# Row scatters of a group queued and issued between units of visits, in a fused convolution and expert-routing kernel

## The chip, the cores and the metric

The kernel runs on one core of one Trainium2 chip. The metric is device time in microseconds (us) of one execution; lower is better. A core has five engines that run side by side, each through its own instruction queue in order: PE (matrix multiply, with PEld for its weight loads), DVE (vector), ACT (scalar), POOL (GpSimd, which here issues indirect transfers) and SP (which here issues plain transfers). They wait for one another through semaphores.

## The reference

```python
# convolution: 7 taps per token, softmax weights per token and head
w = exp(weight_gen - max) ; w = w / (sum(w) + 1e-09)
out = np.einsum('bshk,bskhg->bshg', w, x_unf)      # x_unf: the token and its 6 predecessors
x = out.reshape(B * S, D)                          # 23040 tokens, D = 192
# two-level routing: 4 groups of 4 experts
g_idx = argmax(x @ w_group) ; g_w = its softmax weight
e_idx = argmax(x @ w_expert[g_idx]) ; e_w = its softmax weight
# the expert of each token: w1 192x1024, w2 1024x192
h = np.maximum(x[tokens] @ w1[g, e], 0.0)
out[tokens] = (g_w * e_w)[:, None] * (h @ w2[g, e])
```

## The kernel before

The 23040 tokens are cut into 15 groups of 12 columns of 128 tokens. For each group the front of the kernel (`front`, `softmax`, `conv`, `logits`, `ranks`) computes the convolution on DVE, the routing logits on PE, and on DVE each token's place in a DRAM table `rows` that is sorted by expert. Then POOL scatters the twelve columns into `rows`: `scatter_row`, one indirect transfer of 128 rows of 194 floats each, line L488. In the rows below a scatter is `rows<-xrow,posi`.

The experts' work is cut into visits. A visit takes one, two or three blocks of 128 rows of one expert and is done in units (four for two blocks, eight for three): first matrix product (`gemm1`, L872) into `ph`, ReLU on ACT into `hh` (L878, L883), second product (`gemm2`, L910 to L913) into `py`, then `y` (ACT L919 or DVE), and POOL writes the result rows to their tokens with an indirect transfer `out<-y,xb` (L927), one per block, 189 in all. SP's `load` fetches what a visit needs: its rows `xb` (L744), the weights of the first product `raw` (L757 and L764, three transfers of 512, 256 and 256 KB, called a triple below), and those of the second, `wc` (L768). ACT and DVE then split a triple into the three parts of `wa` (ACT casts L781 and L790, DVE L805).

A table `ROUNDS` says after which group which visits become possible: a round may begin when its group's ranks and the `table` of visits made from them are there. `ready(n)` tells whether visit n's round has come; `arrive` holds the planned time of its rows. The order of the instructions is fixed when the program is written: a planner keeps a clock per engine (`clk`, advanced by `run`), `blocks` runs through the units of all visits, and after each unit `fill` pulls steps of the front until DVE's planned clock is ahead. `pump` issues the loads that are asked for and ready; `need` pulls the front until a visit's round is there. PE, ACT, DVE and SP execute in just that written order. POOL's queue is ordered by the framework's scheduler, from the same program.

In `ranks` the twelve scatters are written one after another, directly behind the last DVE step of the group. After the last group, `table` also writes 16 blocks of padding into `rows` (`rows<-pad`, L543, on POOL).

Of the kernel before, what the change touches and what calls it, by code (L numbers as in the profile page):

```python
# [20 lines left out]
LATE = (1.0, 3.0, 3.0)  # L21
AHEAD = (1.0, 1.0, 2.5)
HURRY = 12
WHOLE = 13
SINGLE = tuple((k,) for k in range(7))
MIXED = ((0, 1), (2,), (3,), (4,), (5,), (6,))
# [11 lines left out]
def conv_moe_kernel(ctx: ExitStack, tc: tile.TileContext, x, wgen, w_group, w_expert, w1, w2, out):  # L38
# [13 lines left out]
    SC = 6  # L52
# [13 lines left out]
    ENDS = [r[0] for r in ROUNDS]  # L66
# [6 lines left out]
    FIRST = ENDS[0]  # L73
# [146 lines left out]

    new_raw = [ring(f"raw{i}", m, [P, n]) for i, (n, m) in enumerate(((F, 2), (F, 2), (NFT * D, 1)))]

    state = {"slots": False, "open": False, "unit": 0, "starve": False, "ph": 0, "hold": False}

    def ph_tile(k, shape):
        return ps_h.tile(shape, F32, name=f"ph{k}")
# [9 lines left out]
    def run(eng, cost, *deps):  # L236
        clk[eng] = max([clk[eng]] + [d + HOP for d in deps]) + cost
        return clk[eng]
# [10 lines left out]
    def round_of(g):  # L249
        return next(r for r in range(NR) if g < ENDS[r])  # L250
# [164 lines left out]
    def ranks(g, o, ls, tls):  # L415
        s0, n = COL[g], WIDTHS[g]
        xrow = o.xrow
        for c, row in enumerate(xrow):
            nc.vector.tensor_copy(out=row.bitcast(I32)[:, :, D + 1:D + 2], in_=ii[:, s0 + c * SC:s0 + (c + 1) * SC].unsqueeze(2))
        yield 0.3  # L420
        yield tls
        ohg, exg = yield from first_max(ls[:, :, 0:G], n, "g")
        sel = rt.tile([P, SG, EG, G], F32, name="sel")[:, 0:n]
        nc.vector.tensor_tensor(
            out=sel, in0=ls[:, :, G:].rearrange("p s (g e) -> p s e g", g=G),
            in1=ohg.unsqueeze(2).broadcast_to([P, n, EG, G]), op=ALU.mult)
        yield 0.3
        le = rt.tile([P, SG, EG], F32, name="le")[:, 0:n, :]
        nc.vector.tensor_reduce(out=le, in_=sel, axis=AX.X, op=ALU.add)
        yield 0.3  # L430
        ohe, exe = yield from first_max(le, n, "e")
        ohs = rt.tile([P, SG, EG], F32, name="ohs")[:, 0:n, :]
        nc.vector.tensor_tensor(out=ohs, in0=ohe, in1=sgn4.broadcast_to([P, n, EG]), op=ALU.mult)
        smg = rt.tile([P, SG, 1], F32, name="smg")[:, 0:n, :]
        nc.vector.tensor_reduce(out=smg, in_=exg, axis=AX.X, op=ALU.add)
        yield 0.26
        oh = rt.tile([P, SG, G, EG], BF16, name="oh")[:, 0:n]
        nc.vector.tensor_tensor(
            out=oh, in0=ohg.unsqueeze(3).broadcast_to([P, n, G, EG]),
            in1=ohs.unsqueeze(2).broadcast_to([P, n, G, EG]), op=ALU.mult)  # L440
        ohf = oh.rearrange("p s g e -> p s (g e)")
        nc.vector.tensor_scalar(out=smg, in0=smg, scalar1=1e-9, scalar2=None, op0=ALU.add)
        yield 0.3
        yield NEXT
        t12 = ps_l.tile([P, 2, SG * NE], F32, name="pl")[:, :, 0:n * NE]
        t1 = t12[:, 0, :].rearrange("p (s e) -> p s e", e=NE)
        t2 = t12[:, 1, :].rearrange("p (e s) -> p e s", e=NE)
        nc.tensor.matmul(t1, lhsT=tri, rhs=ohf, start=True, stop=True)
        nc.tensor.matmul(t2, lhsT=ones, rhs=ohf.rearrange("p s e -> p e s"), start=True, stop=True)
        tt = run("pe", 0.4, clk["dve"])  # L450
        sme = rt.tile([P, SG, 1], F32, name="sme")[:, 0:n, :]
        nc.vector.tensor_reduce(out=sme, in_=exe, axis=AX.X, op=ALU.add)
        yield TINY
        nc.vector.scalar_tensor_tensor(out=smg, in0=sme, scalar=1e-9, in1=smg, op0=ALU.add, op1=ALU.mult)
        yield NEXT
        yield Until(tt + LATE[0])
        pre = rt.tile([P, NE * SG], F32, name="pre")[:, 0:NE * n].rearrange("p (e s) -> p e s", s=n)
        nc.vector.tensor_copy(out=pre[:, :, 1:n], in_=t2[:, :, 0:n - 1])
        nc.vector.tensor_copy(out=pre[:, :, 0:1], in_=cnt)
        yield 0.35  # L460
        for c, row in enumerate(xrow):
            nc.vector.reciprocal(out=row[:, :, D:D + 1], in_=smg[:, c * SC:(c + 1) * SC, :])
        yield TINY
        nc.vector.tensor_tensor_scan(
            out=pre.rearrange("p e s -> p (e s)"), data0=smask[n].rearrange("p e s -> p (e s)"),
            data1=pre.rearrange("p e s -> p (e s)"), initial=0.0, op0=ALU.mult, op1=ALU.add)
        yield 0.3
        rk = sel.rearrange("p s e g -> p s (e g)")
        nc.vector.tensor_tensor(out=rk, in0=pre.rearrange("p e s -> p s e"), in1=t1, op=ALU.add)
        nc.vector.tensor_tensor(out=cnt, in0=pre[:, :, n - 1:n], in1=t2[:, :, n - 1:n], op=ALU.add)  # L470
        yield 0.4
        nc.vector.tensor_tensor(out=rk, in0=rk, in1=ohf, op=ALU.mult)
        yield 0.3
        ps = rt.tile([P, SG], F32, name="pos")[:, 0:n]
        nc.vector.tensor_reduce(out=ps.unsqueeze(2), in_=rk, axis=AX.X, op=ALU.add)
        yield 0.3
        pi = rt.tile([P, SG], I32, name="posi", bufs=2)[:, 0:n]
        nc.vector.scalar_tensor_tensor(out=pi, in0=ps, scalar=-1.0, in1=ps, op0=ALU.mult, op1=ALU.max)
        yield TINY
        for s in range(n):  # L480
            run("pool", 1.28, clk["dve"])
            scatter_row(pi[:, s:s + 1], xrow[s // SC][:, s % SC, :], round_of(g))
        if g + 1 in ENDS:
            yield from table(round_of(g))
        o.routed = True

    def scatter_row(idx, src, r):
        written_once(nc.gpsimd.indirect_dma_start(  # L488
# [11 lines left out]
    tabs, arrive = {}, {}  # L500
# [99 lines left out]
        for h in range(2):  # L600
            nc.gpsimd.dma_start(out=rows[NROW + h * BK:NROW + (h + 1) * BK, :].rearrange("(p t) c -> p t c", t=2), in_=pad2)

    scoring, ranking = [], []
    slow = [[halves(), None]]

    def front():
        side = []
        set_up()
        load_group(1)
        next(slow[0][0])  # L610
        yield from softmax(0)

        def pace(g):
            return 99 if g <= FIRST else HURRY if g < MAIN + 3 else 8 if g in ENDS else 2

        def beside(g, n):
            rush = g >= FIRST and not grp[FIRST - 1].routed
            if g >= FIRST and not rush:
                for q in list(slow):
                    yield from move(slow, q, 1)  # L620
            for q in side[:1]:
                if not rush:
                    yield from move(side, q, 3)
            yield from routing(g)

        def routing(g):
            if ranking:
                yield from move(ranking, ranking[0], pace(g))
            if scoring and (not ranking or g < FIRST):
                yield from move(scoring, scoring[0], pace(g) if scoring[0][2].chunks == 2 or g >= FIRST - 1 else 3)  # L630

        def settle(g):
            while not grp[g].routed:
                qs = ranking or scoring
                q = qs[0]
                yield from move(qs, q, 99)
                if qs and qs[0] is q and q[1] is not None:
                    yield Until(q[1][1]) if q[1][0] == "time" else NEXT

        for g in range(ENDS[-1]):  # L640
            o = grp[g]
            o.routed = False
            scoring.append([logits(g, o), None, o])
            for n, c in enumerate(conv(g, o)):
                yield c
                if n == (2 if state["slots"] else 0) and 1 <= g < ENDS[-1] - 1:
                    load_group(g + 1)
                if n >= (12 if state["slots"] else 4) and not o.ahead and g + 1 < ENDS[-1] and g != FIRST - 1:
                    o.ahead = True
                    side.append([softmax(g + 1), None])  # L650
                yield from beside(g, n)
                if g == FIRST - 1 and n in (7, 8):
                    if n == 7:
                        soft = softmax(FIRST)
                    yield next(soft)
            if g == FIRST - 1:
                for n, c in enumerate(soft):
                    yield c
                    yield from beside(g, n)
            yield from finish_all(side)  # L660
            if g:
                yield from settle(g - 1)
        yield from settle(ENDS[-1] - 1)
# [54 lines left out]
    nmain = len(order)  # L718

    def ready(n):  # L720
        return order[n][:2] in arrive

    def plain(n):
        return order[n][1] == 1
# [207 lines left out]

    def need(n):
        while not ready(n):
            state["starve"] = True
            more = step() is not False
            assert more or ready(n)
        state["starve"] = False
# [13 lines left out]
    def blocks(n0, n1, paced):  # L952
# [92 lines left out]
        for i in range(len(units) + LAG):  # L1045
# [25 lines left out]
            if i < len(units):  # L1071
# [7 lines left out]
                for job in list(jobs):  # L1079
# [7 lines left out]
                    work_split(job)  # L1087
                    did += 1
                state["unit"] += 1
            flush()  # L1090
            if paced:
                fill(clk["pe"] + AHEAD[0 if cur.plain else 1 if cur.o.whole else 2])
# [48 lines left out]
```

## Time and profile before

| | |
|---|---|
| median of 3 runs | 1333.68 us (1323.01 to 1336.16) |
| profiled execution | 1335.81 us |
| its span in the trace | 1334.1 us |
| mean granted clock of PE | 0.951 |
| PE busy | 1192.9 us (89%) |
| DVE busy | 950.5 us (71%) |
| ACT busy | 640.1 us (48%) |
| POOL busy | 455.6 us (34%) |

The profiled execution is 2.1 us above the median. 1.7 us of it lie outside the span. Busy time counts the instructions that compute or issue an indirect transfer; an engine that is not busy is waiting for data, for another engine, or to be given its next instruction. The granted clock of PE has two levels, 2.4 GHz (1.0) and 1.2 GHz (0.5); a mean between them says what share of a stretch was at the lower one.

### The profile page before, as it was taken

The numbers are of one execution on the slowest core, as the hardware profiler recorded it, in microseconds if no ns is written. First come the engines' busy times: TensorE is split into PE (matmuls) and PEld (weight loads), VectorE is DVE, ScalarE is ACT, GpSimd is POOL, SyncE is SP. The second block draws the span as 40 slices with busy tenths as digits, with TensorE's granted clock in tenths as the row PEclk, the third lists the DMA queues.
The fourth block names the chain that finished last, engine by engine and source line by source line (L and its number), as shares of the span: only waits on it lengthen the run. The fifth ranks groups of instructions, "written<-read, shape, count | busy, mean of one in ns | idle before, by whom it ended". The sixth has DMA issues, their size and how long they took to land. (4 is left out here: it accounts for less than half of the span.)

```text
span 1334.1 us, 23736 instructions
## 1 busy us (share of the span) xinstructions
PE 1192.9 (89%) x8165; PEld 1104.5 (83%) x8165; DVE 950.5 (71%) x1660; ACT 640.1 (48%) x1232; POOL 455.6 (34%) x442
## 2 busy tenths in 40 slices
PE   5776877798999999999989798989786999999995
PEld 3444877688998989898989697989686999999995
DVE  8897776768988979798978597888633146655662
ACT  1223334344555555455545454645343466556652
POOL 6232331415253525344533415252416312112221
PEclk9988998788999999899999899999887999999998
DMA  9238789555878767677776666545436665565551
GB/s 258 85 120 275 239 213 287 190 197 172 265 224 278 215 236 225 228 223 253 229 237 213 217 196 209 188 155 168 158 88 216 197 205 149 154 176 165 151 164 39
DMA packets 78851, 261.94 MB, mean 196 GB/s; under 512 B 14669, under 2 KB 29559, under 8 KB 76928
## 3 DMA queue, kind: packets, MB, share of 16 engines
q1 hardware_dynamic: 59544, 220.85, 54.4%
q0 software_dynamic: 19056, 39.20, 8.8%
q8 instruction: 66, 1.08, 0.3%
q14 instruction: 65, 0.53, 0.1%
q10 hardware_dynamic: 120, 0.28, 0.1%
HBM read 216.92 MB, written 44.23 MB: 196 GB/s over the span
## 5 line engine op out<-in xcount | busy, mean ns | idle before, releaser
L872 PE MATMUL ph<-xh,wa 128*128 128x256 f32 (+1 forms) x1896 | 477.0, 321 | 8.1 <-issue 7.4
L910 PE MATMUL py<-wc,hh 128*128 128x192 f32 x2272 | 440.2, 334 | 34.4 <-issue 17.5
L927 POOL DMA_INDIRECT out<-y,xb x189 | 222.1, 1175 | 706.3 <-ACT y L919 449.5
L910 PEld LDWEIGHTS py<-wc,hh 128*128 128x128 f32 x2272 | 379.2, 196 | 40.6 <-issue 22.3
L872 PE MATMUL ph<-xl,wa 128*128 128x256 f32 (+1 forms) x1264 | 360.4, 300 | 8.1 <-issue 8.1
L878 ACT ACTIVATE hh<-ph 128x512 f32<-128x512 f32 (+2 forms) x320 | 175.9, 550 | 366.5 <-PE ph L872 258.4
L872 PEld LDWEIGHTS ph<-xh,wa 128*128 128x128 f32 x1896 | 329.5, 194 | 17.9 <-issue 16.4
L488 POOL DMA_INDIRECT rows<-xrow,posi x180 | 202.1, 1123 | 152.6 <-issue 65.9
L287 DVE TENSOR_TENSOR pr<-xin,wt 128x1152 f32<-128x1152 f32 x186 | 249.0, 1351 | 4.3 <-PE ph L328 2.0
L872 PEld LDWEIGHTS ph<-xl,wa 128*128 128x128 f32 x1264 | 243.4, 193 | 9.5 <-issue 9.5
L305 DVE TENSOR_TENSOR xrow<-xrow,pr 128x1152 f32<-128x1152 f32 x144 | 194.9, 1353 | 0.6
L805 DVE TENSOR_TENSOR wa<-raw,wa 128x1024 fp32r<-128x1024 f32 x79 | 96.5, 1221 | 127.8 <-ACT wa L781 111.7
L805 DVE SCALAR_TENSOR_TENSOR pr<-ph,hh 128x384 fp32r<-128x384 f32 (+1 forms) x120 | 68.8, 574 | 89.0 <-ACT hh L883 84.0
L805 DVE TENSOR_TENSOR xl<-tpx,xh 128x512 fp32r<-128x512 f32 (+1 forms) x99 | 62.8, 634 | 61.5 <-ACT xh L852 50.6
L883 ACT ACTIVATE hh<-ph 128x384 fp32r<-128x384 f32 (+1 forms) x120 | 61.1, 510 | 79.8 <-PE ph L872 70.5
L912 PE MATMUL py<-wc,hh 128*128 128x384 f32 x272 | 87.2, 362 | 0.0
L781 ACT CAST wa<-raw 128x1024 fp32r<-128x1024 f32 x79 | 82.9, 1049 | 7.0 <-DMA raw<-in_moe_w 7.0
L790 ACT CAST wa<-raw 128x1024 fp32r<-128x1024 f32 x79 | 82.8, 1048 | 0.5 <-DMA raw<-w1lo 0.5
L919 ACT ACTIVATE y<-py,xb 128x192 f32<-128x192 f32 x176 | 66.2, 424 | 27.2 <-PE py L910 19.0
L391 ACT COPY xT<-tp 128x384 f32<-128x384 f32 x84 | 40.3, 480 | 78.3 <-PE pl L367 30.5
L913 PE MATMUL py<-wc,pr 128*128 128x192 f32 x272 | 68.4, 251 | 0.0
L852 ACT CAST xh<-tpx 128x512 fp32r<-128x512 f32 (+1 forms) x99 | 53.5, 540 | 3.9 <-PE py L910 1.8
(170 smaller groups left out, 1287.2 us busy)
## 6 DMA issues: line engine op xcount, KB each, us to landing
wc<-in_moe_w SPq DMA_DIRECT2D x73, 768.0 KB
raw<-in_moe_w SPq DMA_DIRECT2D x79, 512.0 KB
xin<-in_x SPq DMA_DIRECT2D x14, 1728.0 KB
raw<-in_moe_w SPq DMA_DIRECT2D x87, 256.0 KB
raw<-w1lo SPq DMA_DIRECT2D x79, 256.0 KB
raw<-in_moe_w SPq DMA_DIRECT2D x17, 768.0 KB
xb<-rows SPq DMA_DIRECT2D x59, 194.0 KB
wa<-in_moe_w SPq DMA_DIRECT2D x22, 384.0 KB
```

What stands on the lines that cost most here:

```text
L287: nc.vector.tensor_tensor(out=dst, in0=o.xin[:, c0 + k:c0 + k + SC, :].rearrange("p s (h g) -> p s h g", g=HG), in1=w4[:, c0:c0 + SC, :, k ...
L305: nc.vector.tensor_tensor(out=acc, in0=acc, in1=prs[k - 2], op=ALU.add)
L488: written_once(nc.gpsimd.indirect_dma_start(out=rows[:, :], out_offset=bass.IndirectOffsetOnAxis(ap=idx, axis=0), in_=src, in_offset=None, ...
L781: nc.scalar.copy(out=o.wa[:, 0, :], in_=o.raw[0])
L790: nc.scalar.copy(out=o.wa[:, 2, :], in_=o.raw[1])
L805: f(*a, **k)
L872: nc.tensor.matmul(ph[:, v, :], lhsT=w[:, f0:f0 + P], rhs=rhs, start=i == 0, stop=i == len(terms) - 1)
L878: nc.scalar.activation(out=hh, in_=ph, func=AF.Relu)
L910: nc.tensor.matmul(b.acc[t], lhsT=hh[:, v, c], rhs=wc[0][:, f, :], start=f == 0 and not (b.wide and t == 1), stop=f == NFT - 1 and not (b. ...
L912: nc.tensor.matmul(b.py[t], lhsT=hh[:, v, c], rhs=wc[f // 4][:, f % 4].rearrange("p l d -> p (l d)"), start=f == 0, stop=False)
L913: nc.tensor.matmul(b.acc[t], lhsT=hl[:, v, c], rhs=wc[f // 4][:, f % 4, 0, :], start=False, stop=f == NFT - 1)
L927: ins = nc.gpsimd.indirect_dma_start(out=out[:, :], out_offset=bass.IndirectOffsetOnAxis(ap=b.x.bitcast(I32)[:, t, D + 1:D + 2], axis=0), ...
```

## The change

The ranks of a group no longer write their twelve scatters; they put them into a list `sending`. For the first two groups the list is emptied at once. For the others `send_due`, called after each unit of a visit, writes one scatter if PE's planned clock has reached `due`, and sets `due` 3.0 us (`GAP`) on. What is left two groups later is written at the top of `front`'s loop, and `need` writes all that is left when a round is awaited. A round counts as ready only when the scatters of its last group are written (`state["sent"]`), and its planned arrival is moved to 7.0 us behind the last of them. Since `ready` stands ahead of every load of a visit, the weights of a new round wait for it as well as the rows do.

```diff
+GAP = 3.0
...
-        for s in range(n):
-            run("pool", 1.28, clk["dve"])
-            scatter_row(pi[:, s:s + 1], xrow[s // SC][:, s % SC, :], round_of(g))
+        sending.extend((g, pi[:, s:s + 1], xrow[s // SC][:, s % SC, :], s == n - 1, clk["dve"]) for s in range(n))
+        if g < FIRST:
+            send_rows()
         if g + 1 in ENDS:
             yield from table(round_of(g))
         o.routed = True
+
+    def send_rows(most=99):
+        while sending and most > 0:
+            g, idx, src, end, at = sending.pop(0)
+            run("pool", 1.28, at)
+            scatter_row(idx, src, round_of(g))
+            most -= 1
+            if end:
+                state["sent"] = g + 1
+                for r, nb in arrive:
+                    if ENDS[r] == g + 1:
+                        arrive[r, nb] = max(arrive[r, nb], clk["pool"] + 7.0)
+
+    def send_due():
+        if sending and state["due"] <= clk["pe"]:
+            send_rows(1)
+            state["due"] = max(state["due"], clk["pe"] - 2.6) + GAP
...
         for g in range(ENDS[-1]):
+            while sending and sending[0][0] < g - 1:
+                send_rows(1)
             o = grp[g]
...
     def ready(n):
-        return order[n][:2] in arrive
+        return order[n][:2] in arrive and state["sent"] >= ENDS[order[n][0]]
...
     def need(n):
         while not ready(n):
+            send_rows()
+            if ready(n):
+                break
             state["starve"] = True
...
                 state["unit"] += 1
+            send_due()
             flush()
```

On POOL, at the scatters of the seventh group, this stands in the queue before (x12 is twelve in a row; the number behind `y` or `xb` is that of the buffer):

```order
L927 DMA out<-y_181,xb_172 23040x192
L927 DMA out<-y_182,xb_172 23040x192
L488 DMA rows<-xrow,posi 188928x194 x12
L927 DMA out<-y_183,xb_173 23040x192
L927 DMA out<-y_184,xb_173 23040x192
L927 DMA out<-y_185,xb_174 23040x192
```

And after, at the same place:

```order
L947 DMA out<-y_181,xb_172 23040x192
L947 DMA out<-y_182,xb_172 23040x192
L506 DMA rows<-xrow,posi 188928x194 x7
L947 DMA out<-y_183,xb_173 23040x192
L947 DMA out<-y_184,xb_173 23040x192
L506 DMA rows<-xrow,posi 188928x194 x5
L947 DMA out<-y_185,xb_174 23040x192
```

Two result writes now stand inside the group's scatters; the scatters are otherwise still next to one another. The first five groups and the fourteenth are where they were. The sixth, eighth and eleventh have all twelve together behind two more writes than before, the thirteenth behind three more. The seventh and the ninth stand as 7 and 5 with two writes between, the tenth and the twelfth as 10 and 2, these behind two more writes for the tenth.

The last group on POOL, before (`pfi` and the ISA rows fetch the address of a block of padding):

```order
L927 DMA out<-y_189,xb_173 23040x192
L488 DMA rows<-xrow,posi 188928x194
L927 DMA out<-y_181,xb_174 23040x192
L927 DMA out<-y_182,xb_174 23040x192
L488 DMA rows<-xrow,posi 188928x194 x11
L541 TENSOR_LOAD pfi
L541 ISA x2
L543 ISA
L543 DMA rows<-pad 256x1x194
```

And after:

```order
L947 DMA out<-y_189,xb_173 23040x192
L947 DMA out<-y_181,xb_174 23040x192
L947 DMA out<-y_182,xb_174 23040x192
L506 DMA rows<-xrow,posi 188928x194 x4
L559 TENSOR_LOAD pfi
L559 ISA x2
L561 ISA
L561 DMA rows<-pad 256x1x194
L947 DMA out<-y_183,xb_172 23040x192
L947 DMA out<-y_184,xb_172 23040x192
```

Four of its scatters stand ahead of the padding, and the other eight now stand behind all of it and two more pairs of writes.

On SP, the loads of visits 66 to 68 before (visit 68 is the first of a new round; `raw_190` and `raw_192` are its triple, `xb_172` is visit 66's rows, and visit 67's rows, `xb_173`, come behind these rows):

```order
L744 DMA xb_172<-rows 128x388
L768 ISA
L768 DMA wc<-in_moe_w 128x1536
L752 TENSOR_LOAD tab_10913
L752 ISA x2
L757 ISA
L757 DMA raw_190<-in_moe_w 128x1024
L764 ISA
L764 DMA raw_192<-in_moe_w 64x1024
L764 ISA
L764 DMA raw_192<-w1lo 64x1024
```

And after:

```order
L788 DMA wc<-in_moe_w 128x1536
L763 TENSOR_LOAD tab_10203
L763 ISA x2
L764 ISA
L764 DMA xb_173<-rows 128x388
L788 ISA
L788 DMA wc<-in_moe_w 128x1536
L772 TENSOR_LOAD tab_10890
L772 ISA x2
L777 ISA
L777 DMA raw_190<-in_moe_w 128x1024
L784 ISA
```

The triple of the new round's first visit has gone behind the rows and second weights of the visit before it. The same exchange stands at visits 14, 16, 19, 31, 42 and 63. On ACT the casts of these triples go later with them: visit 68's first cast stood seven units ahead of the visit and stands four ahead, visit 14's and 19's went from seven to three, and visit 63's from eleven to five. No instruction is added or taken away on PE, ACT, DVE or SP.

## Rows read from the trace of the kernel before

**Rows 1.** Page, part 1: busy us of each engine.

```profile
PE 1192.9 (89%) x8165; PEld 1104.5 (83%) x8165; DVE 950.5 (71%) x1660; ACT 640.1 (48%) x1232; POOL 455.6 (34%) x442
```

**Rows 2.** Stretches: length, busy us of PE, PEld, DVE, ACT, POOL; clock, DMA share.

```profile
447.70:470.70 23.00, 21.42 (x163) 20.21 (x163) 18.76 (x41) 10.65 (x20) 18.13 (x16) 1.00 0.82 242
...
517.80:540.80 23.00, 20.35 (x157) 19.22 (x155) 21.56 (x36) 10.73 (x20) 18.43 (x16) 0.99 0.78 237
...
651.90:675.00 23.10, 20.35 (x156) 19.18 (x154) 21.57 (x36) 10.75 (x20) 18.46 (x16) 1.00 0.75 222
705.00:726.00 21.00, 21.00 (x155) 20.80 (x154) 19.20 (x40) 12.12 (x23) 4.53 (x4) 1.00 0.66 198
726.00:743.80 17.80, 10.75 (x68) 9.46 (x66) 9.74 (x24) 3.47 (x7) 13.67 (x14) 0.84 0.67 207
...
938.00:957.00 19.00, 10.11 (x58) 9.53 (x57) 10.62 (x44) 5.40 (x12) 12.73 (x13) 0.81 0.30 87
996.00:1015.00 19.00, 12.18 (x81) 11.22 (x79) 9.98 (x59) 4.04 (x7) 14.45 (x15) 0.90 0.65 200
1015.00:1036.00 21.00, 17.70 (x91) 17.06 (x92) 4.27 (x6) 9.49 (x19) 11.83 (x16) 0.76 0.68 221
```

**Rows 3.** POOL's timeline, eleventh group: start, length, instruction, idle before.

```profile
726.14 0.97 POOL L488 DMA_INDIRECT rows<-xrow,posi  x1 [5.89 <-DVE units L514]
...
740.23 0.97 POOL L488 DMA_INDIRECT rows<-xrow,posi  x1 [0.30 <-issue]
741.51 0.98 POOL L927 DMA_INDIRECT out<-y,xb  x1 [0.31 <-issue]
```

**Rows 4.** PE's timeline beside the same scatters.

```profile
734.89 0.28 PE L872 MATMUL ph<-xh,wa 128*128 128x256 f32 x1 [0.58 <-issue]
736.33 0.28 PE L872 MATMUL ph<-xl,wa 128*128 128x256 f32 x1 [1.16 <-issue]
```

**Rows 5.** Page, part 5: the group of scatters; busy, mean ns, idle before.

```profile
L488 POOL DMA_INDIRECT rows<-xrow,posi x180 | 202.1, 1123 | 152.6 <-issue 65.9
```

**Rows 6.** POOL's timeline: the last block of padding.

```profile
1037.28 0.68 POOL L543 DMA_DIRECT2D rows<-pad  x1 [0.49 <-issue]
```

**Rows 7.** SP's timeline: the first load of the last round's rows.

```profile
1067.96 0.33 SPq L744 DMA_DIRECT2D xb<-rows  x1
```

**Rows 8.** SP's timeline: the load of visit 62's rows.

```profile
895.10 0.13 SPq L744 DMA_DIRECT2D xb<-rows  x1
```

**Rows 9.** PE's timeline: the first use of these rows.

```profile
897.38 0.33 PE L846 MATMUL tpx<-ident,xb 128*128 128x128 f32 x1 [3.03 <-DMA xb<-rows]
```

**Rows 10.** POOL's timeline, thirteenth group: its first scatter, the first write behind.

```profile
872.47 1.84 POOL L488 DMA_INDIRECT rows<-xrow,posi  x1 [8.30 <-DVE posi L478]
...
890.35 0.98 POOL L927 DMA_INDIRECT out<-y,xb  x1 [0.30 <-issue]
```

**Rows 11.** ACT's timeline: the last y of these writes.

```profile
878.08 0.42 ACT L919 ACTIVATE y<-py,xb 128x192 f32<-128x192 f32 x1 [0.22 <-PE py L910]
```

**Rows 12.** SP's timeline: the first transfer of visit 10's triple.

```profile
198.35 0.33 SPq L757 DMA_DIRECT2D raw<-in_moe_w  x1
```

**Rows 13.** ACT's timeline: the first cast of that triple.

```profile
216.06 1.04 ACT L781 CAST wa<-raw 128x1024 fp32r<-128x1024 f32 x1 [7.02 <-DMA raw<-in_moe_w]
```

**Rows 14.** PE's timeline at the same time.

```profile
218.01 1.65 PE L910 MATMUL py<-wc,hh 128*128 128x192 f32 x4 [6.08 <-ACT y L919]
```

**Rows 15.** SP's timeline: rows of visit 67, triple of visit 69.

```profile
989.62 0.33 SPq L744 DMA_DIRECT2D xb<-rows  x1
...
991.37 0.33 SPq L757 DMA_DIRECT2D raw<-in_moe_w  x1
```

**Rows 16.** ACT's timeline: first casts of visits 68 and 69.

```profile
992.24 1.04 ACT L781 CAST wa<-raw 128x1024 fp32r<-128x1024 f32 x1
...
1005.23 1.05 ACT L781 CAST wa<-raw 128x1024 fp32r<-128x1024 f32 x1
```

**Rows 17.** Page, part 5: the first casts of all triples.

```profile
L781 ACT CAST wa<-raw 128x1024 fp32r<-128x1024 f32 x79 | 82.9, 1049 | 7.0 <-DMA raw<-in_moe_w 7.0
```

More of the change, by code (lines that the diff above doesn't have):

```diff
@@ L221, in conv_moe_kernel @@
     new_raw = [ring(f"raw{i}", m, [P, n]) for i, (n, m) in enumerate(((F, 2), (F, 2), (NFT * D, 1)))]
-    state = {"slots": False, "open": False, "unit": 0, "starve": False, "ph": 0, "hold": False}
+    state = {"slots": False, "open": False, "unit": 0, "starve": False, "ph": 0, "hold": False, "sent": 0, "due": 0.0}
     def ph_tile(k, shape):
@@ L601, in set_up @@
             nc.gpsimd.dma_start(out=rows[NROW + h * BK:NROW + (h + 1) * BK, :].rearrange("(p t) c -> p t c", t=2), in_=pad2)
-    scoring, ranking = [], []
+    scoring, ranking, sending = [], [], []
     slow = [[halves(), None]]
```

## The prediction

> **What bounds the kernel now.** I read the busy times of the page first: PE is the fullest engine, 1192.9 of 1334.1 us [rows 1]. So the room is PE's 141 us of idle time and its stretches at the lower clock, and the question is how much of it belongs to the scatters. The table of stretches says so. Between two groups' scatters PE has no gap at all (21.00 us busy of 21.00 at clock 1.00, from 705 us); in the stretch behind it, which is that of the eleventh group's scatters, it is busy for 10.75 of 17.80 us at 0.84 [rows 2]. POOL's timeline shows what stands there: scatters at 1.28 us apiece, back to back, and two result writes directly behind them [rows 3]. PE's timeline shows the manner of the loss: eight or nine microseconds into the run, single matmuls follow one another with 0.6 and 1.2 us between, and no engine is named as the one waited for, only "issue" [rows 4]. The DMA engines are not full then (share 0.67, and 0.30 beside the fourteenth group's scatters), and POOL is the only engine that works without a break [rows 2]. I can't name the mechanism from the trace; I take it as a price that a back-to-back run on POOL puts on the engines beside it.
>
> **What the scatters cost at most.** Idle PE time in the run stretches: 1.58 (from 447.7 us), 2.65, 2.75, 7.05, 8.89, 6.82 and 3.30 us; together 33.0. At the lower clock, length times (1 - clock): 2.8 + 3.6 + 1.9 + 5.0 = 13.4 us [rows 2]. That is some 46 us for the seventh, eighth, tenth, eleventh, fourteenth and fifteenth groups; the ninth, twelfth and thirteenth should add less than the mean of these, and I take the whole prize as 45 to 65 us.
>
> **What the change does with it, by the order.** The program asks for one scatter per unit at most, 3.0 us apart, but the queue of POOL still holds them together: all twelve, 10 and 2, or 7 and 5. No instruction waits for PE between two scatters, so what is next to each other in the queue is issued every 1.28 us as before [rows 3]. The 1123 ns of a scatter are the same work at another place [rows 5]; POOL, 455.6 us busy, has room for it [rows 1]. So the main term is zero by default, with these corrections:
>
> 1. *Writes ahead of the scatters or inside them* (sixth to thirteenth group). A write that was last in the run becomes first and the run starts when its y is there, but writes and scatters are still some 14 to 16 in a row. The run with two writes ahead (from 447.7 us) left PE idle for 1.58 us, those without (from 517.8 and 651.9 us) for 2.65 and 2.75 [rows 2]: 1.1 us less. Three groups that had none ahead now get them or a pair inside: -3 us. The bounds are 0 and, if a pair inside really breaks the run, half of the 33 us idle.
>
> 2. *The last group.* Four scatters, then padding, then eight scatters. The two stretches from 996 to 1036 us cost 6.82 + 3.30 us idle and 1.9 + 5.0 at the lower clock, 17.0 together [rows 2]. A third of it going with the shorter run is -6 us; bounds 0 and -17. The last eight come 18 to 25 us later, but the last round's rows are not fetched until 1067.96 us, 30 us behind the last padding at 1037.28 [rows 6, 7], so I cost the lateness at nothing; if that cover goes, up to 10 us come back.
>
> 3. *Visit 62's rows.* Its load was issued at 895.10 us and PE waited 3.03 us for it [rows 8, 9]. It needs a buffer that is free when three writes are done, and these stood behind the thirteenth group's scatters: the first at 890.35, though the y of the last was there at 878.5 [rows 10, 11]. All three now go ahead of the scatters. -3.0 us, with little doubt, since POOL starts this group at 872.47 [rows 10] and would only wait some 6 us for the y.
>
> 4. *Later triples.* At a new round the first visit's weights stand behind the previous visit's rows, and so behind the wait of SP for a free row buffer. The row to price a late triple is visit 10's: issued from 198.35 us on, its first cast waited 7.02 us and ran at 216.06, 17.7 us behind the issue [rows 12, 13]; PE then stood still for 6.08 us, since ACT's next y was queued behind that cast [rows 14]. With 3 us for a time at the lower clock behind it (an estimate; stretches above lose 1.9 to 5.0 us each in that way), 9 us a place. Visit 69's triple, issued at 991.37, was cast 13.9 us later without a wait [rows 15, 16]: so a lead of 14 us was enough there, and 17.7 just what it took at visit 10. At visits 14, 16, 19 and 63 the triples were issued further ahead of their casts, and have room to lose. Visit 68 is the tight one: its triple can't be issued before the rows of visit 67, at 989.62, and its cast, at 992.24 before and three units later now, is due at about 1001, with some 3 us a unit [rows 15, 16]. That is a lead of some 11 us where 14 are wanted, and I take +4 us for it, and zero for the others; the bounds are 0 and 9 at each of four places. A gain is excluded: of what the triples let pass, only visit 62's rows were late, and these have a term of their own.
>
> 5. *The planner's own bookkeeping.* Softmax, logits and casts move by one to four units. They have no wait of PE in the stretches between the runs [rows 2], so I cost that at nothing; if a routing step is late, the next group's scatters are too, and their slack is a round.
>
> Sum: -3 - 6 - 3 + 4 = -8 us on the profiled 1335.8, so 1327.8; the median of the runs lies 2.1 below its profiled execution, which makes 1325.7, and I say 1326.
>
> **A rule weighed.** DMA share 0.30 and clock 0.81 stand in one stretch beside the fourteenth group's scatters [rows 2]: PE lost most where the transfers were fewest. The Trainium skill, "DMA: Bandwidth & Descriptors", section "SWDGE vs HWDGE vs iDMA", says that inside each DMA engine the transfers issued by GpSimd and by SP go through different queues, and the engine takes turns between them. By that rule the spacing of scatters changes nothing for the loads beside them, terms 1 and 2 are zero, and the sum is 1334.7. The trace doesn't contradict that; it only shows that something other than the loads' bandwidth is what PE lacks.
>
> **The rivals.**
>
> *A, the runs really break.* A pair of writes inside, waiting for its own y, or the padding between, gives the other engines their pause, and half of the prize comes back: 25 to 35 us, so about 1301 us; all of it would be some 1280. For it: the stall starts only after some 8 us of scatters (726.14 to 734.89) and a run of seven takes 9 us [rows 3, 4]. Against it: seven of the ten groups from the sixth on still have ten to twelve in a row.
>
> *B, the weights come late.* The wait at visit 10 is what each boundary could become: SP issues the new round's triple only after a row buffer is free, the cast on ACT stands in front of `y`, and PE stops for that. It decides where a triple is issued less than 14 us (18 if visit 10 is the measure) ahead of its cast [rows 12 to 16]. Visits 16, 19, 63 and 68 with 9 us each are 36 us; three of them, and none of the gains of terms 1 and 2, give 1333.7 + 27 - 3 = 1358. For it: this is the one thing that the order shows plainly on SP and ACT, and the casts moved too, which saves ACT from waiting but not the visit behind. Against it: only one of 79 triples was late before, the 7.0 us of visit 10 being all that these first casts ever waited for [rows 17].
>
> *C, the change doesn't do what it says.* The scatters are as packed as before, the time is the same but for terms 3 and 4: 1335. Its outcome is hard to tell from the forecast and is counted with it.
>
> **How the numbers follow.** A measurement of this kernel can tell about 1% (13 us) from no change. Forecast and C 0.46, A 0.33, B 0.21. Of the first, 0.03 pass the 1% bound on either side; 0.02 of A and 0.02 of B stay within it. So faster by over 1% (under 1320) 0.33 + 0.03 - 0.02 = 0.34, slower (over 1347) 0.21 + 0.03 - 0.02 = 0.22, within 1% 0.44. The likeliest case by itself spans 1316 to 1340: term 2 from 0 to -17 and term 4 from 0 to +9. The range reaches into A to 1296, which leaves out the third of it in which most of the prize comes back, and into B to 1352, which leaves out the half with three late places or more: some 0.1 at either side.
>
> **What would show it.** The group of scatters keeps its mean near 1.1 us and its 1.28 us pitch; POOL's timeline still has runs of 12 or more, and beside them PE waits for "issue" as now. Term 2: PE idle in the last group's two stretches falls from 10.1 us by a few. Term 3: the 3.03 us wait for visit 62's rows is gone. Term 4: ACT's wait for `raw` has new places at visit 68, perhaps 16 and 19, beyond the 7.0 us of visit 10. I am wrong on the fast side if PE is full beside the groups that stand as 7 and 5, and on the slow side if ACT's waits for `raw` sum to over 15 us.

## The result, and the profile after

The changed kernel takes 1344.04 us (median of 7 runs, 1339.61 to 1350.77) against 1330.93 us (1323.01 to 1336.16): a ratio of 1.0118, 95% interval 1.0083 to 1.0153. It is slower by 1.2%, some 16 us by that ratio, which compares all runs, and 13.1 us by the medians; 8 us of gain had been forecast. Its profiled execution took 1349.91 us, with a span of 1348.3 and a mean granted clock of 0.945.

From the page of the changed kernel, the row of busy times and four groups (those of [rows 1, 5, 17], and two more):

```profile
PE 1193.9 (89%) x8165; PEld 1109.1 (82%) x8165; DVE 950.6 (71%) x1660; ACT 640.1 (47%) x1232; POOL 449.6 (33%) x442
...
L947 POOL DMA_INDIRECT out<-y,xb x189 | 218.1, 1154 | 738.8 <-ACT y L939 484.9
...
L506 POOL DMA_INDIRECT rows<-xrow,posi x180 | 200.1, 1111 | 139.5 <-issue 64.3
...
L810 ACT CAST wa<-raw 128x1024 fp32r<-128x1024 f32 x79 | 82.7, 1046 | 3.2 <-DMA raw<-w1lo 3.2
L801 ACT CAST wa<-raw 128x1024 fp32r<-128x1024 f32 x79 | 82.8, 1048 | 0.0
```

No engine works more than 1.0 us longer than before; the span grew by 14.2 us, and PE is idle for 154.4 us where it was for 141.2. The scatters cost what they cost (1111 ns against 1123). The casts don't wait for late weights: the 7.0 us of visit 10 [rows 17] are gone, and 3.2 us for the last part of a triple is all there is.

The stretches beside the scatters of the sixth, tenth, twelfth, thirteenth and fifteenth group in the changed kernel (columns as in [rows 2]):

```profile
390.60:413.00 22.40, 11.55 (x72) 11.14 (x72) 9.43 (x30) 4.93 (x9) 13.72 (x14) 0.73 0.49 155
...
678.60:702.00 23.40, 14.38 (x98) 14.02 (x98) 11.47 (x28) 7.82 (x15) 14.92 (x14) 0.84 0.50 161
...
820.00:843.00 23.00, 15.30 (x98) 13.89 (x97) 11.02 (x44) 7.25 (x13) 15.05 (x14) 0.81 0.52 171
901.00:922.00 21.00, 11.41 (x65) 11.06 (x64) 12.93 (x49) 3.54 (x8) 15.83 (x15) 0.87 0.59 179
...
1024.00:1042.00 18.00, 13.83 (x87) 12.94 (x86) 12.81 (x61) 8.61 (x15) 13.13 (x15) 0.92 0.62 197
```

These are the stalls of [rows 2], for the most part at other groups. The sixth group's stretch now lacks 10.9 us of PE, the tenth's 9.0 (2.75 before, from 651.9 us), the thirteenth's 9.6. The fifteenth's lacks 4.2.

How a stall looks, in the thirteenth group's scatters. POOL's timeline of the changed kernel, from the last write ahead to the last scatter:

```profile
903.69 1.13 POOL L947 DMA_INDIRECT out<-y,xb  x1 [0.31 <-issue]
905.12 0.98 POOL L506 DMA_INDIRECT rows<-xrow,posi  x1 [0.30 <-issue]
...
920.25 0.97 POOL L506 DMA_INDIRECT rows<-xrow,posi  x1 [0.30 <-issue]
```

PE's timeline there:

```profile
908.89 0.34 PE L892 MATMUL ph<-xl,wa 128*128 128x384 f32 x1
...
910.73 0.33 PE L892 MATMUL ph<-xl,wa 128*128 128x384 f32 x1
920.65 2.29 PE L930 MATMUL py<-wc,hh 128*128 128x192 f32 x6 [9.59 <-ACT hh L898]
```

And ACT's:

```profile
905.79 0.37 ACT L872 CAST xh<-tpx 128x256 fp32r<-128x256 f32 x1
920.11 0.49 ACT L898 ACTIVATE hh<-ph 128x384 f32<-128x384 f32 x1 [13.95 <-remote]
```

By these rows PE has finished its last two products `ph` by 909.2 and 911.1 us and waits for ACT's `hh`. ACT has been idle since 906.2 and starts that `hh` at 920.11; the view says "remote", which is to say that the signal came just then, but that no recorded instruction that could have sent it had ended just before. Each engine waits for the other although PE's work is done: the signal of PE reached ACT nine microseconds or more late, as the run of scatters came to its end. The stalls before the change have the same marks. I use the waits of ACT that end in "remote" or "issue" as their measure below: 113.9 us in the kernel before, 134.6 after. Of the fifteen such waits of more than 5 us in the two traces, thirteen end within 3 us of the end of a run of transfers on POOL.

### The profile page after: what moved, and what is told of

It is laid out like the page before. It is cut to its first block, busy times and chain, and to the rows that moved or that the text cites. A ratio compares the mean times of both kernels' runs of the same rounds, so it can differ in the third digit from the quotient of the medians.

```text
span 1348.3 us, 23734 instructions
## 1 busy us (share of the span) xinstructions
PE 1193.9 (89%) x8165; PEld 1109.1 (82%) x8165; DVE 950.6 (71%) x1660; ACT 640.1 (47%) x1232; POOL 449.6 (33%) x442
## 2 busy tenths in 40 slices
DMA packets 78851, 261.94 MB, mean 194 GB/s; under 512 B 14669, under 2 KB 29559, under 8 KB 76928
## 4 chain that ended last, share of the span: by engine, by line
PE 57%; issue 17%; DMA 7%; DVE 6%; another core or an unknown queue 4%; POOL 4%; ACT 4%; POOLq 1%; SPq 0%; ACTq 0%; DVEq 0%
PE ph L892 23%; PE py L930 21%; DVE pr L288 3%; POOL out L947 3%; DMA xb<-rows 2%; PE pl L368 2%; PE py L932 1%; DMA out<-y,xb 1%; PE tpx L867 1%; PE tp L385 1%; PE ph L329 1%; PE tpx L866 1%; DMA rows<-xrow,posi 1%; ACT hh L898 1%
## 5 line engine op out<-in xcount | busy, mean ns | idle before, releaser
L947 POOL DMA_INDIRECT out<-y,xb x189 | 218.1, 1154 | 738.8 <-ACT y L939 484.9
L506 POOL DMA_INDIRECT rows<-xrow,posi x180 | 200.1, 1111 | 139.5 <-issue 64.3
L867 PE MATMUL tpx<-ident,xd 128*128 128x128 f32 x178 | 47.7, 290 | 26.2 <-ACT xd L850 12.3
```

Of the source, the lines that this page charges most:

```text
L506: written_once(nc.gpsimd.indirect_dma_start(out=rows[:, :], out_offset=bass.IndirectOffsetOnAxis(ap=idx, axis=0), in_=src, in_offset=None, ...
L947: ins = nc.gpsimd.indirect_dma_start(out=out[:, :], out_offset=bass.IndirectOffsetOnAxis(ap=b.x.bitcast(I32)[:, t, D + 1:D + 2], axis=0), ...
```

## The experiments

The chips differed, and the numbers can't be read without that. On two of those on which the experiments ran (called clean below) the kernel before takes 1249 us; on the two others, and where the result above was measured, 1328 to 1333 (called chips with stalls below). Each ratio is to the kernel before on the same chip.

**Weights that don't wait, on a clean chip.** `ready` asks for the scatters only where rows are loaded:

```diff
-    def ready(n):
-        return order[n][:2] in arrive and state["sent"] >= ENDS[order[n][0]]
+    def ready(n, part=0):
+        return order[n][:2] in arrive and (part > 0 or state["sent"] >= ENDS[order[n][0]])
...
```

(The rest of the edit hands the part of the load on to `ready`.) Expected: 

> The changed kernel, but only the rows of a new round wait for its scatters; its weights are issued as soon as the tables of the round are known, as before. Theory runs (the loss sits beside the unbroken runs of POOL's transfers, and the change only moved these against the visits): POOL's queue is packed as in the changed kernel, so the time stays near it, 1335 to 1350 us, and the stalls sit beside the runs. Rival gating (the loss comes from the loads and casts of a new round that now come later): the time goes back to that of before, 1325 to 1335.

Measured: 1245.59 us, ratio 0.9981 (0.9950 to 1.0013). The level was missed altogether, and so nothing was told of the stalls: there were none. It is not a test of the weights alone either. The edit also moved POOL's queue: the two writes that free the row buffer of visit 69 stand behind 3 scatters and 7 blocks of padding, behind 4 and 1 in the changed kernel, and PE waits 6.97 us for that visit's rows.

**POOL in program order, on a clean chip.** POOL is added to the engines whose order is fixed:

```diff
-    ctx.enter_context(tc.manual_schedule(engines={ET.PE, ET.Activation, ET.DVE, ET.SP}))
+    ctx.enter_context(tc.manual_schedule(engines={ET.PE, ET.Activation, ET.DVE, ET.SP, ET.Pool}))
```

Expected: 

> The changed kernel with POOL's queue in the order in which the program is written, so that scatters really stand between the result writes of visits (at most 8 or 9 in a row in place of 12). Theory runs: shorter runs stall less, the idle PE time beside the scatters falls by a third or more and the time comes to 1300 to 1325. Rival gating: SP, ACT and PE are as in the changed kernel, so the time stays at 1338 to 1350.

Measured: 1248.69 us, 0.9991 (0.9959 to 1.0023). Both edits together, on the other clean chip. Expected: 

> The changed kernel with both edits of the first experiments: POOL's queue in program order, and weights that don't wait for scatters. On a chip without stalls neither has anything to win back and the ratio is 0.99 to 1.00; on a chip with stalls the theory of runs expects 0.95 to 0.985, the rival 0.99 to 1.00.

Measured: 1245.34 us, 0.9963 (0.9940 to 0.9987), as said for a chip without stalls.

**A copied index, which spaces the scatters for real.**

```diff
+            if g >= FIRST:
+                own = rt.tile([P, 1], I32, name="own", bufs=12)
+                nc.vector.tensor_copy(out=own, in_=idx)
+                at, idx = run("dve", 0.1), own
             run("pool", 1.28, at)
             scatter_row(idx, src, round_of(g))
```

On the first clean chip. Expected: 

> The changed kernel with one more small DVE instruction per scatter, a copy of its column of indices written at the place where the scatter is queued; the scatter reads the copy and so can't be issued before the units ahead of it are through on DVE. Theory runs: the runs break for real where scatters were meant to be apart (four or so), what is left are the eight that are flushed when a round is needed; stalls fall, 1300 to 1325. Rival gating: 1338 to 1350, plus a little for 156 more DVE instructions (some 0.1 us each, off the path).

Measured: 1253.10 us, 1.0039 (1.0016 to 1.0061). On the second clean chip. Expected: 

> The changed kernel with the copied indices, which spaces the scatters for real. On a chip without stalls 1.000 to 1.008 as in its first run; on a chip with stalls the theory of runs expects 0.95 to 0.985.

Measured: 1254.20 us, 1.0043 (1.0022 to 1.0064). Without stalls the spacing only costs.

**Twice the time on POOL, on a clean chip.** The kernel before, in POOL's program order, with three memsets behind every scatter:

```diff
...
             scatter_row(pi[:, s:s + 1], xrow[s // SC][:, s % SC, :], round_of(g))
+            if g >= FIRST:
+                for _ in range(3):
+                    nc.gpsimd.memset(junk, 0.0)
```

Expected: 

> The kernel before, with POOL's queue in program order and three small memsets on POOL behind every scatter from the third group on (some 1 us in all), so that a group's twelve take about 28 us in place of 15 to 18. No engine waits for the memsets but POOL. Theory runs: with half the rate of transfers the late signals vanish, PE idle beside the scatters falls by 20 us or more; writes behind the scatters are later by 12 us, which costs some of it; 1300 to 1325. Rival (the stalls come from POOL being occupied at all, or from the number of transfers): the stalls last as long as the scatters do, longer than before, 1340 to 1370.

Measured: 1304.49 us, 1.0444 (1.0423 to 1.0465): slower, as the rival had it, by more than it said (its 1340 to 1370 were at most 1.03 of the kernel before), and not by its reason. There are no stalls in it. A group's twelve scatters take 29 to 35 us from the third group on, where they took 16 to 19, and PE waits for rows that are loaded late. From the view of PE's waits in this kernel (us in total, times, longest), and from ACT's timeline:

```profile
PE tpx L850 <- DMA xb<-rows: 40.8, 5, 19.1
PE tp L386 <- ACT rem L378: 23.7, 8, 16.3
```

```profile
927.62 0.41 ACT L834 COPY xd<-xb 128x256 f32<-128x256 f32 x1 [14.98 <-DMA xb<-rows]
```

The longest wait of the second row ends at 929.44 us and is of the same kind: ACT's `rem` stood in its queue behind that `xd`. So late writes keep row buffers from being loaded; that is what a slower POOL costs where nothing else is wrong. Program order was not tried on the kernel before without the memsets; on the changed kernel it costs nothing (0.9991).

**Both kernels, unchanged, on a clean chip.** Expected of the kernel before: 

> The kernel before, unchanged, for a trace of it on the chip of these experiments, where its runs took 1249 us and not 1331. If the stalls beside the scatters (PE waiting for nothing that the trace names, ACT for signals that PE had long sent) make the difference between the two chips, they are absent here, although the scatters stand in the same unbroken runs; then an unbroken run is not enough for a stall. If they are there, the difference lies elsewhere.

Measured: 1246.87 us for this one run, span 1245.3. Stretches of it beside the eleventh, fourteenth and fifteenth group's scatters:

```profile
667.60:690.00 22.40, 22.40 (x178) 21.97 (x177) 20.51 (x33) 13.10 (x25) 16.83 (x16) 1.00 0.84 266
...
859.00:882.00 23.00, 23.00 (x157) 22.53 (x157) 19.86 (x52) 11.06 (x23) 15.24 (x15) 1.00 0.44 131
906.00:940.00 34.00, 21.77 (x137) 20.59 (x136) 13.62 (x64) 10.63 (x19) 24.35 (x27) 0.82 0.66 203
```

Where [rows 2] has 10.75 of 17.80 and 10.11 of 19.00, PE is full, beside the same twelve scatters in a row. An unbroken run is thus not enough for a stall; something in which these chips differ is needed too. Of these three only the last group has a loss here. Over the whole span PE is busy for less time too, at a mean granted clock of 0.974, where [rows 1] has 1192.9 us at 0.951:

```profile
PE 1155.7 (93%) x8165; PEld 1080.3 (87%) x8165; DVE 949.5 (76%) x1660; ACT 640.1 (51%) x1232; POOL 447.4 (36%) x442
```

Expected of the changed kernel: 

> The changed kernel, unchanged. Theory runs: what it lost by was the stalls beside POOL's runs; on a chip that shows none it is as fast as before, a ratio of 0.995 to 1.005. Rival gating: later loads and casts cost on any chip, a ratio of 1.008 to 1.015 here too.

Measured: 1236.94 us, 0.9909 (0.9880 to 0.9939): **faster** than the kernel before by 0.9%, and by 10.2 us of span in the two traces. That is better than my theory's own number, and the opposite of what the rival said. By the first use of each visit's rows on PE, the changed kernel is 2.7 us ahead at visit 65, 9.0 at 66, 3.3 at 68, 12.0 at 69 and 10.2 from 74 on. So most of it is won at visit 69. The load of its rows waits for two writes. In the kernel before, these and the load stand here, on POOL and on SP:

```profile
928.77 1.04 POOL L927 DMA_INDIRECT out<-y,xb  x1 [1.72 <-issue]
```

```profile
932.70 0.34 SPq L744 DMA_DIRECT2D xb<-rows  x1
```

In the changed kernel, the same two rows:

```profile
915.80 1.01 POOL L947 DMA_INDIRECT out<-y,xb  x1 [0.30 <-issue]
```

```profile
920.48 0.33 SPq L764 DMA_DIRECT2D xb<-rows  x1
```

PE's longest wait for rows was 11.2 us before and is 2.9 after. Eight scatters that stood ahead of the writes stand behind the padding now.

**The last group alone, and all but the last, on a chip with stalls.** The list is emptied at once for other groups, by the condition in `ranks`:

```diff
-        if g < FIRST:
+        if g < len(WIDTHS) - 1:
```

Expected: 

> The changed kernel with the list emptied at once for every group but the last, so only the last group's scatters are queued. By the order the two writes that free visit 69's row buffer then stand behind 3 scatters and 7 blocks of padding, where they stood behind 11 and 3 before and behind 4 and 1 in the changed kernel. Theory writes (without stalls the gain is that result writes which free a row buffer stand further ahead): about a third of the 8 us that the changed kernel won at visit 69, -2 to -5 us, 0.995 to 0.999. Theory that the split of the last group by itself makes the gain (a shorter run): -8 us, 0.993. On a chip with stalls: 0.99 to 1.01.

Measured: 1328.64 us, 0.9988 (0.9952 to 1.0024). And with `g < FIRST or g == len(WIDTHS) - 1`. Expected: 

> The changed kernel with the last group's scatters sent at once and all others queued. The order puts its twelve together, with the two writes directly behind them and ahead of all padding. Theory writes: visit 62's term as in the changed kernel (-3 us), and the writes for visit 69 stand behind 12 transfers in place of 14, -2 to -4 us; together 0.994 to 0.997. If only the split of the last group counted: 0.998 to 1.000. On a chip with stalls 1.00 to 1.02, as the changed kernel had there.

Measured: 1351.56 us, 1.0154 (1.0117 to 1.0190). The loss belongs to the groups ahead of the last: they alone lose as much as the whole change, as far as the intervals can tell, and the last group alone loses nothing.

**The copied index on the same chip.** Expected: 

> The changed kernel with the copied indices, which really spaces the scatters, once more, for the case that this chip shows stalls: then the theory of runs expects 0.95 to 0.985 and the rival 1.00 to 1.015. On a chip without stalls 1.002 to 1.006, as in its two runs there.

Measured: 1282.02 us, 0.9642 (0.9586 to 0.9698). The kernel that costs 0.4% on clean chips wins 3.6% here. The view of POOL's waits (us in total, times, longest) shows scatters that wait for their copy on DVE, and the timeline one of them:

```profile
POOL rows L510 <- DVE own L493: 49.5, 23, 7.4
```

```profile
501.57 1.70 POOL L510 DMA_INDIRECT rows<-xrow,own  x1 [7.44 <-DVE own L493]
```

And ACT's waits for signals, in this kernel first, then in the one with all but the last group queued (us in total, times, longest):

```profile
ACT hh L902 <- issue: 20.2, 15, 2.0
ACT hh L902 <- remote: 19.1, 7, 4.5
```

```profile
ACT hh L898 <- remote: 100.5, 14, 15.0
...
ACT hh L898 <- issue: 14.1, 12, 1.9
```

Over all of ACT's lines it is 59.5 us in place of 142.1. The twelve scatters of a group from the third on take 22 to 46 us here, where they take 15 to 21 in the changed kernel (the last group, 41, apart).

**Copies for some groups, on another chip with stalls.** The condition ahead of the copy becomes `3 <= g < len(WIDTHS) - 1`. Expected: 

> The changed kernel with copied indices for the fourth to the fourteenth group; the last group is queued as in the changed kernel, so that the two writes for visit 69 stand ahead of nearly all padding. On a chip with stalls the theory of runs expects 0.955 to 0.97, a little under the 0.964 of the kernel that copies everywhere, by the 8 us won at visit 69. On a chip without stalls the gain of the changed kernel (0.991) less what the spacing costs at the fourth group, 0.992 to 1.000. Rival gating: 1.00 to 1.015 on either.

Measured: 1286.02 us, 0.9668 (0.9598 to 0.9739). ACT's "remote" and "issue" are 49.7 us. The gain at the last group didn't come with it: PE still waits 14.2 us for visit 69's rows, because the two writes for it stand behind all sixteen blocks of padding in this kernel's queue, and not ahead of them as I had expected. From `4 <= g`. Expected: 

> The same with copies from the fifth to the fourteenth group. By the order the middle groups stand in pieces of four or less more often, but the writes for visit 69 come behind 4 scatters and 6 blocks of padding. With stalls 0.955 to 0.97; without, 0.992 to 1.000, since the fourth group's delay is gone and half of the gain at visit 69 with it.

Measured: 1317.26 us, 0.9887 (0.9804 to 0.9970): a miss. By the order its groups from the fifth on are in pieces much like those of the kernel just ahead, and yet ACT's unexplained waits are 99.8 us. The fourth group, unbroken again, has 9.0 of them; and one wait of 7.5 us ends beside a run of six transfers and a seventh 0.8 us behind it. One wait of PE for rows is 10.9. Expected of the changed kernel beside them: 

> The changed kernel unchanged, beside the two above on the same chip. With stalls 1.008 to 1.016 as in the first measurement; without 0.988 to 0.994 as in its second run.

Measured: 1350.56 us, 1.0136 (1.0058 to 1.0213), as at first; ACT's unexplained waits are 136.4 us. On this one chip, then, the copies for the fourth to the fourteenth group take 64.5 us off the changed kernel.

**By group and by run.** I added ACT's "remote" and "issue" waits that end inside an unbroken run of transfers on POOL (less than 0.7 us between two) or within 5 us of its end, in the eight traces from chips with stalls. Over nine tenths of such waits lie there. By group, in us (S a scatter, o a write, p padding):

```
group     before                    changed kernel
 6        SSSSSSSSSSSSoooo   5.5    ooSSSSSSSSSSSS    13.6
 7        ooSSSSSSSSSSSSoo   4.6    SSSSSSSooSSSSSoo   2.8
 8        SSSSSSSSSSSSoooo   6.2    ooSSSSSSSSSSSSoo   0
 9        ooSSSSSSSSSSSSoo   0      SSSSSSSooSSSSSoo   9.8
10        SSSSSSSSSSSSoooo   7.8    SSSSSSSSSSooSS    14.9
11        SSSSSSSSSSSSoo    15.5    ooSSSSSSSSSSSSoo   6.9
12        ooSSSSSSSSSSSSoo  11.3    SSSSSSSSSSooSS    15.1
13        SSSSSSSSSSSSooo    0      oooSSSSSSSSSSSS   17.5
14        SSSSSSSSSSSS       9.9    SSSSSSSSSSSSooo    0
sum                         60.8                      80.6
```

This is no chance of one execution: the sixth, tenth, twelfth and thirteenth group, 24.6 us together before and 61.1 after, have 62.6 in the trace with all but the last group queued, 63.0 in the third trace of the changed kernel, and 18.6 where only the last group is queued.

In the eight traces a run of 1 to 3 transfers has 0.2 us of these waits on average (467 runs), of 4 to 6, 1.4 (34), of 7 to 9, 1.6 (12), of 10 to 12, 3.8 (21), of 13 or 14, 9.8 (37), of 15 or 16, 4.8 (38). Of the runs of twelve and more, those that end in a scatter have 12.4 us (19), those that end in two or more writes 4.3 (52). But fifteen of these 19 are five groups seen in three traces of one order (the same up to the last group), and on the clean chip, from the same order, the changed kernel's runs at the sixth, tenth, twelfth and thirteenth group all end in two or three writes. So a scatter at the end is what a stall leaves, since it keeps the next `y` away; that it is a cause is not shown.

## Why the prediction was wrong

*What bounds the kernel:* right. The losses beside the scatters are what separates the chips with stalls from the clean ones: the kernel before spans 1334.1 and 1245.3 us, 88.8 apart, of which I had seen 45 to 65. The 88.8 split into 51.6 us of idle PE and 37.2 us in which PE is busy for longer; counted as the prediction counts it, length times (1 - clock), the lower clock costs 33 us more on the chip with stalls (65 against 32). I had 33.0 and 13.4 of these from seven stretches, and left out the groups ahead of the sixth.

*"So the main term is zero by default":* **this step failed.** I read from the order that the runs are as packed as before, and took it that their price is the same. The runs are as packed, but the price isn't. The changed kernel's spans on the two kinds of chip, 1348.3 and 1235.1, are 113.2 apart: by these four traces the stalls grew by 24.4 us where I had costed nothing, and ACT's unexplained waits by 20.7. Without stalls the change is worth -10.2, the difference on a clean chip. 24.4 - 10.2 is the 14.2 of the spans.

*Term 1 (writes ahead or inside, -3):* wrong in sign. From the sixth to the thirteenth group ACT's unexplained waits went from 50.9 to 80.6 us. I had inferred the 1.1 us from three rows of groups whose runs all ended in writes; it was never a measure of writes ahead. The count was off too: five groups (the sixth, eighth, tenth, eleventh and thirteenth) had no write ahead and got some, not three. Why a group at its new place stalls for longer is not shown. The run by itself doesn't set it: the fourteenth stands where it was in POOL's order, and its 9.9 us went to nothing.

*Term 2 (the last group, -6):* right in sign and near in size, in part by luck. On a clean chip, where there were no stalls to shrink (ACT's unexplained waits are 0.9 us in all), visit 69 comes 8.7 us earlier against visit 68, since two writes that free its row buffer no longer stand behind eleven scatters; the term had no such gain in it. Where the result was measured the same stretch, from visit 68 to 69, shrank by 10.0 us, and ACT's unexplained waits at the last group fell from 11.1 to 3.6, so the shorter run that I named may have a part there. The two weren't separated.

*Term 3 (visit 62, -3):* the wait of 3.03 us [rows 9] is gone, but nothing is won by it. On the clean chip visit 62 gains 5.6 us on visit 61, where 60 and 61 had lost 3.3 and 2.0 (PE now waits 2.37 us for visit 60's rows); at visit 59 as at 65 the changed kernel is some 2.7 us ahead. The three writes that free visit 62's rows went ahead, and the visits about it shifted by as much; I haven't traced why.

*Term 4 (late triples, +4) and rival B:* zero. No first cast waits; rival B, to which I gave the chance of being slower, is refuted by that row and by the clean chip, where the written order of loads and casts is the same and the kernel is faster. The sign that I had named for the slow side, waits for `raw` of over 15 us, didn't show (3.2 us); the kernel was slower by the term that I had put at nothing.

*Rival A:* the mechanism is right, but this change doesn't do it. Breaking the runs for real wins 3.3 to 3.6% on chips with stalls (44 to 48 us, more than the 25 to 35 that I gave it, which was itself a little over half of 45 to 65). It takes a wait for another engine's progress, here DVE's; a planner's clock leaves POOL free to issue one scatter behind the other.

*The rule weighed:* with terms 1 and 2 at zero the sum was 1334.7, and 1344 was measured; the time went into late signals. The rule itself (the Trainium skill, "DMA: Bandwidth & Descriptors", section "SWDGE vs HWDGE vs iDMA") says nothing of these, and no run here tests it.

*The spread:* the low end of the likeliest case doesn't follow from its terms. Term 2 at -17 with the others as forecast gives 1314.7, not 1316.

**What stays open.** What differs between the chips, and what holds the signals back there. No run tells whether it is the chip itself or something beside the kernel on it. That the signal is late, and not PE's own end, is read from the rows of a trace in which the ends of matmuls are modelled. Spacing the scatters matters (the copies show it), but the kernel with copies from the fifth group on, in like pieces by the order, kept 99.8 us of waits where the changed kernel has 136.4 on the same chip, and runs of 15 or 16 lose less than runs of 13 or 14. Where in a visit the run falls may decide it; no experiment separated that.

## What to carry to other kernels

A planner's order spaces nothing on an engine that has no wait: to spread transfers in time, give each of them something to wait for. Before costing a moved run at zero, compare what like runs cost at different places in the kernel: here twelve scatters in a row cost from 0 to 15.5 us of waits, by the group. And look which result writes free a buffer, since a few transfers ahead of them were worth 8.7 us on a clean chip. Time such a change on more than one chip: its sign was not the same on two.

## What the runs showed of the hardware

The same kernel takes 1249 us on some chips and 1331 us on others, with the same 261.94 MB moved and like instruction times (a scatter takes 1145 and 1123 ns on the mean). In the traces they differ in the granted clock of PE (0.974 and 0.951 on the mean) and in the arrival of signals between engines, mostly while POOL issues ten or more indirect transfers in a row: an `hh` on ACT that waits 13.95 us, nine of them behind PE's last matmul for it, and nothing of the kind on a clean chip, where all waits of ACT without a recorded cause sum to 0.9 us.
